# Small products of the attention weights moved to quarters of the array, regrouped through memory

## Chip, cores, metric

One core of a Trainium2 chip. The metric is the device time of one execution in microseconds (us). Every number below is from a run or a profile; a number worked out from others says how. Engines in the profile: PE (matmul), PEld (its weight loads), DVE (vector), ACT (scalar), POOL, and SP, whose queue (SPq) issues nearly all transfers. PSUM is the memory that the matmuls of this kernel write to; it is handed out in banks, here often in pairs. A transfer has landed when the semaphore that reports its end is complete.

## The reference

Two linear-attention blocks A and B read the same input `x` (2048 x 640), each with 32 heads of 20 columns; a sigmoid gate mixes them.

```python
qkv = (x @ wqkv) ...                      # per block: q, k, v
pq, pk = phi(q), phi(k)                   # phi(t) = where(t > 0, t + 1, exp(t)) + 1e-6
kv  = einsum("bhsd,bhse->bhde", pk, v)    # 20 x 20 per head
num = einsum("bhqd,bhde->bhqe", pq, kv);  den = einsum("bhqd,bhd->bhq", pq, z)[..., None] + 1e-6
a   = (num / den) ... @ wo
return g * a + (1 - g) * b
```

## The kernel before

Since `num @ wo` is `pq @ (kv @ wo)`, the kernel makes W' = blockdiag(kv) @ wo (640 x 640) once per block. The output is then pq, scaled by gate over denominator, times W', summed over both blocks. PE runs, in this order: K of both blocks; the Gram products G of A, with Q products as filler; G of B, with Q products, **kv and W' of A** as filler; partial sums of A (one per 128 rows of output, "o_part"), with **kv and W' of B** among them; then the products with W' of B ("o_rest") and the last rows.

The parts that matter (cuts marked `# ...`):

```python
GR = 120; NU = 6                       # six heads = 120 rows; six units per block
def kv_unit(X):                        # kv of six heads in one 120x120 block, then masked to the block diagonal
    for us in ((0, 1, 2, 3), (4, 5)):
        # PE: 5 matmuls per unit, moving 120 columns each
        # DVE: KVL[:, us, (m g)] = PS[:, (u g m)] * mask        (one copy for 4 units, one for 2)
def wp_unit(X, u):                     # one unit of W': 120 rows x 640 columns
    ps = Buf("wp", "ps", 2)            # one pair of PSUM banks
    e.matmul(a[0:GR, 0:512], KVL[X][:, u, :], WO[X][:, u, 0:512], start=True, stop=True)
    e.matmul(a[0:GR, 512:D], KVL[X][:, u, :], WO[X][:, u, 512:D], start=True, stop=True)
    # ins=[bkvl[X][u // 4], ...]: waits for its own masked copy only
    # ACT copies the 120 x 640 result to WST, then one transfer spreads it over WP:
    dma("SP", ..., WP[X][lo // 5 : hi // 5, :, :], WST[X][r:GR, u, :], ...)
# ...
o_part(0); o_part(1); o_part(2); den("B"); o_part(3); kv_unit("B"); o_part(4)
for u in range(NU):
    wp_unit("B", u)
    if u % 2 == 0: o_part(5 + u // 2)
for t in range(8, NOA): o_part(t)      # NOA = 13
for t in range(NOA): o_rest(t)         # first use of W' of B
```

All engines are driven by a small scheduler in the kernel: PE keeps the order of the program, and the order on DVE, ACT and the queue comes from a simulation with modelled costs. Each engine then runs its list strictly in order. `den` makes the denominators: per 512 rows a transfer with transpose, three DVE steps (reduce, reciprocal, factor) and a transpose back.

Of the kernel before, what the change touches and what calls it, by code (L numbers as in the profile page):

```python
# [11 lines left out]
D = 640  # L12
# [7 lines left out]
NU = 6  # L20

# [7 lines left out]
def _consts():  # L29
    p = np.arange(128)[:, None]  # L30
    bd = (p // 20 == np.arange(24)[None, :] // 4).astype(np.float32)
    return _bf16_bits(bd)


CW = 24
# [4 lines left out]
class Buf:  # L40


    def __init__(self, name, pool=None, n=1):
        self.name, self.pool, self.n = name, pool, n
        self.writers, self.readers = [], []
        self.slot = None
        self.war = []
# [25 lines left out]
class Sched:  # L73
# [14 lines left out]
    def run(self):  # L88
# [10 lines left out]
        def can(o, t):  # L99

            w = t
            if o.behind is not None and o.behind.start is None:
                return None
            for d in o.deps:
                if d.end is None:
                    return None
                w = max(w, d.end + (HOP if d.eng != o.eng or d.dma else 0.0))
            for b in o.outs:
                if b.pool and b.slot is None:
                    got = self.pick(b, w)  # L110
                    if got is None:
                        return None
                    w = max(w, got[0])
            return w

        n = len(self.ops)
        while len(self.order) < n:
# [25 lines left out]
            if o.dma:  # L143
                at[e] = w + o.dma[0]
                o.end = max(w + o.dma[0] + 1500.0, bus[0]) + o.dma[1] / o.dma[2]
                bus[0] = o.end
            else:
                o.end = at[e] = w + o.cost
                if e == "PE":
                    o.end += 160.0  # L150
# [14 lines left out]
    def pick(self, b, t):  # L165
# [3 lines left out]
        for x in pool:  # L169
            have[x[1]] = x[0]  # L170
        if b.n == 1:
            if not pool:
                return None
# [3 lines left out]
        c = [(max(have[s], have[s + 1]), s) for s in have if s % 2 == 0 and s + 1 in have]  # L177
# [80 lines left out]
def body(nc, A_x, A_wqkv, A_wo, B_x, B_wqkv, B_wo, gate_w, out, log=None):  # L258
# [17 lines left out]
    WV = {X: sb("WV" + X, [128, NC, D], bf) for X in XS}  # L276
    WO = {X: sb("WO" + X, [GR, NU, D], bf) for X in XS}
# [19 lines left out]
    KVL = {X: sb("KVL" + X, [GR, NU, GR], bf) for X in XS}  # L297
    WST = {X: WKW[0:GR, i * NU * D : (i + 1) * NU * D].rearrange("p (u f) -> p u f", u=NU) for i, X in enumerate(XS)}
# [5 lines left out]
    NOA = 13  # L304
    OA = [XNf[:, 2048 + 1280 * i : 3328 + 1280 * i].bitcast(f32) for i in range(6)]
    OA += [PK["B"][:, 1280 * i : 1280 * i + 1280].bitcast(f32) for i in range(7)]
# [22 lines left out]
    BDM = CST[0:GR, 0:24]  # L329
# [9 lines left out]
    def dma(q, name, dst, src, nbytes, ins=(), outs=(), after=(), issue=450.0, transpose=False, prio=None):  # L339
        def fn(e):  # L340
# [4 lines left out]
        o = op(q, fn, 0.0, ins, outs, after, prio=prio, name=name, dma=(issue, nbytes, 95.0 if transpose else 330.0))  # L345
# [24 lines left out]
    bwo = {X: Buf("wo" + X) for X in XS}  # L370
# [15 lines left out]
    zgw = op("POOL", lambda e: e.memset(GWZ[:, :], 0.0), 200.0, name="zgw")  # L386
    bxo = Buf("xo")
# [8 lines left out]
    def xt_dma(t0, t1):  # L396
# [7 lines left out]
            issue=(t1 - t0) * 850.0,  # L404
# [22 lines left out]
    for X in XS:  # L427
        dma("SP", "wv" + X, WV[X][:, :, :], w3(X, 2), 819200, outs=[bwv[X]])
    for X in XS:
        bo5 = Buf("wo5" + X)  # L430
        dma("SP", "wo" + X, WO[X][:, 0:5, :], wo[X][0:600, :].rearrange("(u p) n -> p u n", p=GR), 768000, outs=[bwo[X]])
        dma("SP", "wo5" + X, WO[X][:, 5, :], wo[X][520:640, :], 153600, outs=[bo5])
        bwo[X, 5] = bo5
# [176 lines left out]
    def g_unit(X, g, fill):  # L610
        ps = Buf("g", "ps", 2)
        i = XS.index(X)
        for t in range(NT):
# [30 lines left out]
            issue=850.0,  # L644
# [6 lines left out]
    def kv_unit(X):  # L651
        gv = GS[X][:, :, :].rearrange("p c (g m) -> p c g m", g=NC)
        for us in ((0, 1, 2, 3), (4, 5)):
            ps = Buf("kv", "ps")

            def fn(e, us=us, ps=ps):
                for i, u in enumerate(us):
                    lo = GR * u if u < 5 else D - GR
                    for c in range(NC):
                        r = e.matmul(  # L660
                            PS[0:GR, ps.slot, GR * i : GR * i + GR],
                            WV[X][:, c, lo : lo + GR],
                            gv[:, c, :, lo // 5 : lo // 5 + 24],
                            start=(c == 0),
                            stop=(c == NC - 1),
                        )
                return r

            o = op("PE", fn, 5 * len(us) * mm_cost(GR), ins=[bwv[X]] + [bgs[X, g] for g in range(NC)], outs=[ps], name="kv" + X)
            if X == "A":  # L670
                kv_op[X].append(o)
            b = Buf("kvl")
            bkvl[X].append(b)
            n = len(us)
            op(
                "DVE",
                lambda e, us=us, ps=ps, n=n: e.tensor_tensor(
                    out=KVL[X][:, us[0] : us[0] + n, :].rearrange("p u (m g) -> p u g m", g=NC),
                    in0=PS[0:GR, ps.slot, 0 : GR * n].rearrange("p (u g m) -> p u g m", u=n, g=NC),
                    in1=BDM.unsqueeze(1).unsqueeze(1).to_broadcast([GR, n, NC, 24]),  # L680
                    op=ALU.mult,
                ),
                dve1(GR * n),
# [6 lines left out]
    bwp = {}  # L690
    bwpm = {X: [] for X in XS}

    def wp_unit(X, u):
        ps = Buf("wp", "ps", 2)

        def fn(e):
            a = psw(ps, D)
            e.matmul(a[0:GR, 0:512], KVL[X][:, u, :], WO[X][:, u, 0:512], start=True, stop=True)  # L698
            return e.matmul(a[0:GR, 512:D], KVL[X][:, u, :], WO[X][:, u, 512:D], start=True, stop=True)  # L699

        op(
            "PE",
            fn,
            mm_cost(512) + mm_cost(128),
            ins=[bkvl[X][u // 4], bwo[X] if u < 5 else bwo[X, 5]],
            outs=[ps],
            name="wp%s%d" % (X, u),
        )
        b = Buf("wst")
        op(  # L710
            "ACT",
            lambda e: e.activation(WST[X][:, u, :], psw(ps, D)[0:GR, :], ACT.Copy),
            act_cost(D),
            ins=[ps],
            outs=[b],
            prio=-1,
            name="wpc",
        )
        bwp[X, u] = b
        d = Buf("wpm")  # L720
        bwpm[X].append(d)
        r = 80 if u == 5 else 0
        lo, hi = GR * u, min(D, GR * u + GR)
        dma(
            "SP",
            "wpm%s%d" % (X, u),
            WP[X][lo // 5 : hi // 5, :, :],
            WST[X][r:GR, u, :],
            1280 * (hi - lo),
            ins=[b],  # L730
            outs=[d],
            issue=850.0,
            prio=-1,
        )
# [85 lines left out]
    def den(X):  # L820

        i = XS.index(X)
        for b in range(NB):
# [10 lines left out]
                issue=900.0,  # L834
# [40 lines left out]
                issue=900.0,  # L875
# [112 lines left out]
    def fill_b(g):  # L988
        def f(k):
# [14 lines left out]
            elif g == 2:  # L1004
                q_next(1)
                wp_unit("A", 2 * k)
                wp_unit("A", 2 * k + 1)
            elif g == 3:
                q_next(2)
# [12 lines left out]
    den("B")  # L1022
    o_part(3)
    kv_unit("B")
    o_part(4)
    for u in range(NU):
        wp_unit("B", u)
        if u % 2 == 0:
            o_part(5 + u // 2)
# [52 lines left out]
```

## Time and profile before

| | before |
|---|---|
| median time, first three runs | 188.76 us |
| PE busy | 98% of the span |
| PE waits in all | 0.7 us |
| W' on PE, both blocks | 12 units of 0.27 us = 3.3 us |
| kv on PE | 30 matmuls, 1.65 us per block |

First the page: span, busy time by engine, then the busy tenths and the granted PE clock in 40 equal slices, then the chain that ended last.

```profile
span 187.6 us, 3202 instructions
PE 184.6 (98%) x1261; PEld 107.9 (58%) x1261; DVE 135.4 (72%) x260; ACT 95.6 (51%) x171; POOL 0.8 (0%) x8
...
PE   8999999999999999999999999999999999999995
...
PEclk9999999999999999999999999999999999999999
...
PE 96%; DMA 2%; SPq 0%; DVE 0%; issue 0%; DVEq 0%
```

PE is the limit from end to end, at full clock (9 means 90% or more; the mean of this profile is 1.000). A gain must take time out of PE's stream, and any new wait of PE is a loss. The view of waits for PE confirms it: columns are who waited, for whom, total us, times, longest.

```profile
PE ps L444 <- DVE ONE L372: 0.4, 1, 0.4
PE ps L513 <- DMA WKW<-in_A_wqkv_dram: 0.3, 1, 0.3
```

The timeline of PE around the first W' unit of B (start us, duration us, engine, line, operation):

```profile
147.00 0.38 PE L698 MATMUL ps<-WOB,KVLB 120*120 120x512 bf16 x1
147.22 0.22 PE L699 MATMUL ps<-WOB,KVLB 120*120 120x128 bf16 x1
147.27 0.65 PE L904 MATMUL ps<-WPA,EX 128*128 128x512 bf16 x3
```

Durations overlap in the pipeline, so the cost of a unit is read from starts: 147.27 - 147.00 = 0.27 us.

The masked copies of kv of B on DVE, and the issue times of the six transfers that spread W' of B (minimum, median, maximum ns; first and last start):

```profile
L677 DVE TENSOR_TENSOR KVLB<-ps,CST x2: 908/1204/1499, 145.3 to 146.5; 120x480 bf16<-120x480 f32 x1, 120x240 bf16<-120x240 f32 x1
...
L343 SPq DMA_DIRECT2D WPB<-WKW x6: 689/772/792, 150.1 to 155.5; - x6
```

### The profile page before, as it was taken

Reading aid. Unit: us, or ns where it says so; the run is one execution under the profiler, and the core shown is the slowest. Engines: PE = TensorE matmul, PEld = TensorE weight load, DVE = VectorE, ACT = ScalarE, POOL = GpSimd, SP = SyncE. Lnnn points to the kernel's source line nnn. Section 1 sums busy time; section 2 is a strip of 40 time slices with the busy share of each in tenths; the row PEclk is TensorE's granted clock in tenths of the full one; section 3 lists DMA queues with packets and bytes.
Section 4 is the critical chain, followed back from the end, with each engine's and each line's share of the span. In section 5 each row is a group of like instructions: output and inputs, shape, how many; then the busy total and the mean of one; then the engine's idle time right before and its main releaser. Section 6 shows DMA issues by size and latency. Waiting matters only on the chain.

```text
span 187.6 us, 3202 instructions
## 1 busy us (share of the span) xinstructions
PE 184.6 (98%) x1261; PEld 107.9 (58%) x1261; DVE 135.4 (72%) x260; ACT 95.6 (51%) x171; POOL 0.8 (0%) x8
## 2 busy tenths in 40 slices
PE   8999999999999999999999999999999999999995
PEld 4555555555555656665557556655556655555552
DVE  2388888888833555487798999879996999965600
ACT  5365655556554546544675667877524594100012
POOL 1000000000000000000000000000000000000000
PEclk9999999999999999999999999999999999999999
DMA  7999999996001011011701222540015165132322
GB/s 185 293 163 158 252 392 364 344 214 136 4 0 35 0 38 35 0 35 24 92 10 31 56 49 48 124 116 3 0 35 118 32 153 134 39 140 105 136 79 70
DMA packets 36301, 19.89 MB, mean 106 GB/s; under 512 B 25630, under 2 KB 36286, under 8 KB 36286
## 3 DMA queue, kind: packets, MB, share of 16 engines
q1 hardware_dynamic: 35844, 19.48, 41.6%
q8 instruction: 10, 0.16, 0.4%
q10 hardware_dynamic: 442, 0.20, 0.4%
q14 instruction: 5, 0.04, 0.1%
HBM read 9.39 MB, written 2.62 MB: 64 GB/s over the span
## 4 chain that ended last, share of the span: by engine, by line
PE 96%; DMA 2%; SPq 0%; DVE 0%; issue 0%; DVEq 0%
PE ps L904 23%; PE ps L744 23%; PE ps L513 18%; PE ps L618 18%; PE ps L619 5%; PE ps L514 5%; DMA WKW<-in_A_wqkv_dram 2%; PE ps L660 2%; PE ps L698 1%; SPq L343 0%; PE ps L699 0%; DVE TSB L948 0%; DVEq L230 0%; PE ps L494 0%
## 5 line engine op out<-in xcount | busy, mean ns | idle before, releaser
L513 PE MATMUL ps<-WKW,XT 128*128 128x512 bf16 x160 | 44.4, 381 | 0.3 <-DMA WKW<-in_A_wqkv_dram 0.3
L761 ACT ACTIVATE EK<-ps 128x512 bf16<-128x512 f32 x40 | 23.9, 598 | 31.5 <-PE ps L744 29.4
L514 PE MATMUL ps<-WKW,XT 128*128 128x128 bf16 (+1 forms) x160 | 35.2, 220 | 0.0
L546 ACT ACTIVATE EK<-ps 128x640 bf16<-128x640 f32 x32 | 22.4, 704 | 10.8 <-DVE EK L549 5.9
L513 PEld LDWEIGHTS ps<-WKW,XT 128*128 128x128 bf16 x160 | 15.7, 98 | 19.8 <-DMA WKW<-in_A_wqkv_dram 0.6
L744 PE MATMUL ps<-XT,WQA 128*128 128x512 bf16 x100 | 24.5, 379 | 0.0
L744 PE MATMUL ps<-XT,WQB 128*128 128x512 bf16 x100 | 23.7, 379 | 0.0
L618 PE MATMUL ps<-XN,PKB 128*128 128x512 bf16 x80 | 23.5, 379 | 0.0
L618 PE MATMUL ps<-XN,PKA 128*128 128x512 bf16 x80 | 23.5, 379 | 0.0
L771 DVE TENSOR_SCALAR EK<-EK 128x512 bf16<-128x512 bf16 x40 | 11.6, 291 | 14.9 <-ACT EK L761 14.8
L619 PE MATMUL ps<-XN,PKA 128*128 128x129 bf16 x80 | 17.6, 220 | 0.0
L619 PE MATMUL ps<-XN,PKB 128*128 128x129 bf16 x80 | 17.6, 220 | 0.0
L904 PE MATMUL ps<-WPA,EX 128*128 128x512 bf16 x120 | 17.3, 299 | 0.0
L904 PE MATMUL ps<-WPB,PKA 128*128 128x512 bf16 x120 | 16.5, 299 | 0.0
L744 PEld LDWEIGHTS ps<-XT,WQB 128*128 128x128 bf16 x100 | 10.9, 117 | 8.5
L514 PEld LDWEIGHTS ps<-WKW,XT 128*128 128x128 bf16 x160 | 15.8, 98 | 0.0
L549 DVE TENSOR_SCALAR EK<-EK 128x640 bf16<-128x640 bf16 x32 | 10.4, 326 | 7.1 <-ACT EK L546 7.1
L744 PEld LDWEIGHTS ps<-XT,WQA 128*128 128x128 bf16 x100 | 10.6, 117 | 8.1
L618 PEld LDWEIGHTS ps<-XN,PKA 128*128 128x128 bf16 x80 | 9.4, 118 | 7.9
L618 PEld LDWEIGHTS ps<-XN,PKB 128*128 128x128 bf16 x80 | 9.4, 117 | 7.8
L950 ACT ACTIVATE TSB<-ps 128x640 bf16<-128x640 f32 (+1 forms) x3 | 2.0, 668 | 23.2 <-PE ps L904 23.2
L557 DVE SCALAR_TENSOR_TENSOR PKA<-ps,EK 128x640 bf16<-128x640 f32 x16 | 13.2, 825 | 0.6
(77 smaller groups left out, 239.9 us busy)
## 6 DMA issues: line engine op xcount, KB each, us to landing
out_dram<-TSB SPq DMA_DIRECT2D x15, 160.0 KB, 1.8
XN<-in_A_x_dram SPq DMA_DIRECT2D x1, 2240.0 KB, 9.0
WKW<-in_A_wqkv_dram SPq DMA_DIRECT2D x5, 160.0 KB, 4.2
WKW<-in_B_wqkv_dram SPq DMA_DIRECT2D x5, 160.0 KB, 4.0
WQA<-in_A_wqkv_dram SPq DMA_DIRECT2D x1, 800.0 KB, 10.7
WQB<-in_B_wqkv_dram SPq DMA_DIRECT2D x1, 800.0 KB, 11.9
WVA<-in_A_wqkv_dram SPq DMA_DIRECT2D x1, 800.0 KB, 12.7
WVB<-in_B_wqkv_dram SPq DMA_DIRECT2D x1, 800.0 KB, 14.3
```

Source lines behind the costliest of these rows:

```text
L513: e.matmul(a[:, 0:512], l, WK[X][:, c, 0:512], start=(c == 0), stop=(c == NC - 1))
L514: return e.matmul(a[:, 512:w], l, WK[X][:, c, 512:w], start=(c == 0), stop=(c == NC - 1))
L546: op("ACT", lambda e: e.activation(EK[:, ek.slot, :], psw(ps, D), ACT.Exp), act_cost(D), ins=[ps] + first, outs=[ek], name="ke")
L549: lambda e: e.tensor_scalar(EK[:, ek.slot, :], EK[:, ek.slot, :], 1.0, EPS, op0=ALU.min, op1=ALU.add),
L557: lambda e: e.scalar_tensor_tensor(PKt[X][:, t, :], psw(ps, D), 0.0, EK[:, ek.slot, :], op0=ALU.max, op1=ALU.add),
L618: e.matmul(a[:, 0:512], l, XN[:, t, 0:512], start=(t == 0), stop=(t == NT - 1))
L619: return e.matmul(a[:, 512 : D + 1], l, XN[:, t, 512 : D + 1], start=(t == 0), stop=(t == NT - 1))
L660: r = e.matmul(PS[0:GR, ps.slot, GR * i : GR * i + GR], WV[X][:, c, lo : lo + GR], gv[:, c, :, lo // 5 : lo // 5 + 24], start=(c == 0), st ...
L744: r = e.matmul(PS[:, ps.slot, :], WQ[X][:, c, g::5], XT[:, c, 512 * b : 512 * b + 512], start=(c == 0), stop=(c == NC - 1),)
L761: lambda e: e.activation(EQ[:, eq.slot, :], PS[:, ps.slot, :], ACT.Exp),
L771: lambda e: e.tensor_scalar(EQ[:, eq.slot, :], EQ[:, eq.slot, :], 1.0, EPS, op0=ALU.min, op1=ALU.add),
L904: r = e.matmul(a[:, l0 - lo : h0 - lo], PQ[X, b][:, g, 128 * (t % 4) : 128 * (t % 4) + 128], WP[X][:, g, l0:h0], start=(X == first and g = ...
```

## The change

Three heads at a time need only a 60 x 60 block of kv, so four such products fit on the four 64 x 64 quarters of the array at once. W' is made in two bursts per block, each with half the columns of all eleven products (ten of 60 rows, one of 40). `wo` is loaded at offsets 4 and 64 to fit the quarters, with zero padding. Since a quarter holds 60 rows, the eleven pieces are no longer spread one by one: five stores write W' to memory, and one load brings it back in the layout of WP. Fourteen partial sums of A are kept instead of 13, to give PE more to do while W' of B travels. The scheduling model gets other numbers for transposes.

```diff
+HR = 60; HALF = 320
-        o = op(..., dma=(issue, nbytes, 95.0 if transpose else 330.0))          # and issue=850.0 or 900.0 for transposes
+        timing = (330.0, 1500.0) if not transpose else (140.0, 1500.0) if loading else (1000.0, 1150.0)   # and issue=1250.0
-    NOA = 13
+    NOA = 14
 # kv: WV padded to 128 columns per unit; the sixth unit moves 40 columns instead of 120; three masked copies (480, 120, 40 columns)
+    def wp_burst(X, half):
+        ps = [Buf("wp", "ps", 2) for _ in range(2)]          # two pairs of banks at once
+        for k in range(3):
+            for a, b in ((0, 192), (192, HALF)) if k == 1 else ((0, HALF),):
+                for t in range(4 * k, min(4 * k + 4, 11)):
+                    c, r, u = t // 2 % 2, t % 2 if t < 10 else 1, t // 2
+                    # matmul on quarter (row half r, column half c)
+        op("PE", fn, 640.0, ins=bkvl[X] + ..., outs=ps)      # waits for all three masked copies
+        # two ACT copies of 124 x 960; after the second burst 2 + 3 stores (st), then:
+            dma("SP", "wpl" + X, WP[X][:, :, :], WPD[X].rearrange("(p g) n -> p g n", g=NC), 819200, ins=bwps[X], ...)
-    o_part(3); kv_unit("B"); o_part(4); six wp_units among o_part(5) to o_part(7)
+    kv_unit("B"); o_part(3); wp_burst("B", 0); o_part(4); o_part(5); wp_burst("B", 1); o_part(6); o_part(7)
 # ... (padding, memsets on POOL, split loads of wo, PSUM picking for two pairs)
```

More of the change, by code (lines that the diff above doesn't have):

```diff
@@ L20 @@
 NU = 6
+HR = 60
+HALF = 320
 def _bf16_bits(a):
@@ L30, in _consts @@
     p = np.arange(128)[:, None]
-    bd = (p // 20 == np.arange(24)[None, :] // 4).astype(np.float32)
-    return _bf16_bits(bd)
-CW = 24
+    q, m = p % 64, np.arange(24)[None, :]
+    bd = np.where(p < 64, (q >= 4) & ((q - 4) // 20 == m // 4), (q < 60) & (3 + q // 20 == m // 4))
+    be = q // 20 == m[:, 0:8] // 4
+    return _bf16_bits(np.concatenate([bd, be], axis=1).astype(np.float32))
+CW = 32
 XS_W = 672
@@ L40, with __init__ @@
 class Buf:
-    def __init__(self, name, pool=None, n=1):
-        self.name, self.pool, self.n = name, pool, n
+    def __init__(self, name, pool=None, n=1, at=(0, 2, 4, 6)):
+        self.name, self.pool, self.n, self.at = name, pool, n, at
         self.writers, self.readers = [], []
@@ L107, in can @@
                 w = max(w, d.end + (HOP if d.eng != o.eng or d.dma else 0.0))
+            skip = set()
             for b in o.outs:
                 if b.pool and b.slot is None:
-                    got = self.pick(b, w)
+                    got = self.pick(b, w, skip)
                     if got is None:
@@ L113, in can @@
                     w = max(w, got[0])
+                    skip |= set(range(got[1], got[1] + b.n))
             return w
@@ L144, in run @@
                 at[e] = w + o.dma[0]
-                o.end = max(w + o.dma[0] + 1500.0, bus[0]) + o.dma[1] / o.dma[2]
+                o.end = max(w + o.dma[0] + o.dma[3], bus[0]) + o.dma[1] / o.dma[2]
                 bus[0] = o.end
@@ L163, in run, with pick @@
         return max(o.end for o in self.ops)
-    def pick(self, b, t):
+    def pick(self, b, t, skip=()):
         pool = self.free[b.pool]
@@ L169, in pick @@
         for x in pool:
-            have[x[1]] = x[0]
+            if x[1] not in skip:
+                have[x[1]] = x[0]
         if b.n == 1:
-            if not pool:
+            if not have:
                 return None
@@ L176, in pick @@
             return best[0], best[3]
-        c = [(max(have[s], have[s + 1]), s) for s in have if s % 2 == 0 and s + 1 in have]
+        c = [(max(have[i] for i in range(s, s + b.n)), s) for s in b.at if all(i in have for i in range(s, s + b.n))]
         return min(c) if c else None
@@ L275, in body @@
     WQ = {X: sb("WQ" + X, [128, NC, D], bf) for X in XS}
-    WV = {X: sb("WV" + X, [128, NC, D], bf) for X in XS}
-    WO = {X: sb("WO" + X, [GR, NU, D], bf) for X in XS}
+    WV = {X: sb("WV" + X, [128, NC, D + 8], bf) for X in XS}
+    WO = {X: sb("WO" + X, [128, NU, D], bf) for X in XS}
     PK = {X: sb("PK" + X, [128, NT * D], bf) for X in XS}
@@ L296, in body @@
     GS = {X: sb("GS" + X, [128, NC, D], bf) for X in XS}
-    KVL = {X: sb("KVL" + X, [GR, NU, GR], bf) for X in XS}
-    WST = {X: WKW[0:GR, i * NU * D : (i + 1) * NU * D].rearrange("p (u f) -> p u f", u=NU) for i, X in enumerate(XS)}
+    KVL = {X: sb("KVL" + X, [128, NU, GR], bf) for X in XS}
+    WST = {X: WKW[:, i * NU * D : (i + 1) * NU * D].rearrange("p (u f) -> p u f", u=NU) for i, X in enumerate(XS)}
     WP = {X: sb("WP" + X, [128, NC, D], bf) for X in XS}
@@ L303, in body @@
     FXT = {"A": WV["A"][:, :, :].rearrange("p c f -> p (c f)")[:, 0:2048].rearrange("p (b s) -> p b s", b=NB), "B": XNf[:, 0:2048].rearrange("p (b s) -> p b s", b=NB)}
-    NOA = 13
+    NOA = 14
     OA = [XNf[:, 2048 + 1280 * i : 3328 + 1280 * i].bitcast(f32) for i in range(6)]
-    OA += [PK["B"][:, 1280 * i : 1280 * i + 1280].bitcast(f32) for i in range(7)]
+    OA += [PK["B"][:, 1280 * i : 1280 * i + 1280].bitcast(f32) for i in range(8)]
     NEK, NEQ, NOS = 4, 4, 4
@@ L328, in body @@
     IDN = sb("IDN", [128, 128], bf)
-    BDM = CST[0:GR, 0:24]
+    BDM = CST[:, 0:24]
+    BDE = CST[64:104, 24:32]
     sch = Sched({"ps": 8, "ek": NEK, "eq": NEQ, "os": NOS})
@@ L343, in fn @@
                 return e.dma_start(d, src() if callable(src) else src, transpose=transpose)
-        o = op(q, fn, 0.0, ins, outs, after, prio=prio, name=name, dma=(issue, nbytes, 95.0 if transpose else 330.0))
+        o = op(q, fn, 0.0, ins, outs, after, prio=prio, name=name, dma=(issue, nbytes) + timing)
         if loading:
@@ L369, in body @@
     bwv = {X: Buf("wv" + X) for X in XS}
-    bwo = {X: Buf("wo" + X) for X in XS}
+    bwo = {}
     op("DVE", lambda e: e.memset(ONE[:, :], 1.0), 120.0, outs=[bone], name="one")
@@ L386, in body @@
     zgw = op("POOL", lambda e: e.memset(GWZ[:, :], 0.0), 200.0, name="zgw")
+    bpad = {X: Buf("pad") for X in XS}
+    for X in XS:
+        op("POOL", lambda e, X=X: e.memset(WV[X][:, :, 0:4], 0.0), 100.0, outs=[bpad[X]], prio=10**6, name="wvpad")
+        op("POOL", lambda e, X=X: e.memset(WO[X][0:4, 0:5, :], 0.0), 1500.0, outs=[bpad[X]], prio=10**6, name="wopad")
     bxo = Buf("xo")
@@ L403, in xt_dma @@
             outs=bxt[t0:t1],
-            issue=(t1 - t0) * 850.0,
+            issue=(t1 - t0) * 1250.0,
             transpose=True,
@@ L427, in body @@
     for X in XS:
-        dma("SP", "wv" + X, WV[X][:, :, :], w3(X, 2), 819200, outs=[bwv[X]])
+        dma("SP", "wv" + X, WV[X][:, :, 4 : D + 4], w3(X, 2), 819200, outs=[bwv[X]])
     for X in XS:
-        bo5 = Buf("wo5" + X)
-        dma("SP", "wo" + X, WO[X][:, 0:5, :], wo[X][0:600, :].rearrange("(u p) n -> p u n", p=GR), 768000, outs=[bwo[X]])
-        dma("SP", "wo5" + X, WO[X][:, 5, :], wo[X][520:640, :], 153600, outs=[bo5])
-        bwo[X, 5] = bo5
+        for r in range(2):
+            bwo[X, r] = Buf("wo")
+            dma(
+                "SP",
+                "wo%s%d" % (X, r),
+                WO[X][4 + HR * r : 64 + HR * r, 0:5, :],
+                wo[X][0:600, :].rearrange("(u r p) n -> r p u n", r=2, p=HR)[r],
+                384000,
+                outs=[bwo[X, r]],
+            )
+        bwo[X, 2] = Buf("wo")
+        dma("SP", "wo2" + X, WO[X][64:104, 5, :], wo[X][600:640, :], 51200, outs=[bwo[X, 2]])
     loading.clear()
@@ L643, in g_unit @@
             outs=[bgs[X, g]],
-            issue=850.0,
+            issue=1250.0,
             transpose=True,
@@ L652, in kv_unit, with out @@
         gv = GS[X][:, :, :].rearrange("p c (g m) -> p c g m", g=NC)
-        for us in ((0, 1, 2, 3), (4, 5)):
-            ps = Buf("kv", "ps")
-            def fn(e, us=us, ps=ps):
-                for i, u in enumerate(us):
-                    lo = GR * u if u < 5 else D - GR
-                    for c in range(NC):
-                        r = e.matmul(
-                            PS[0:GR, ps.slot, GR * i : GR * i + GR],
-                            WV[X][:, c, lo : lo + GR],
-                            gv[:, c, :, lo // 5 : lo // 5 + 24],
-                            start=(c == 0),
-                            stop=(c == NC - 1),
-                        )
-                return r
-            o = op("PE", fn, 5 * len(us) * mm_cost(GR), ins=[bwv[X]] + [bgs[X, g] for g in range(NC)], outs=[ps], name="kv" + X)
-            if X == "A":
-                kv_op[X].append(o)
+        def out(src, u0, n, w, mask, r0, r1):
             b = Buf("kvl")
             bkvl[X].append(b)
-            n = len(us)
             op(
                 "DVE",
-                lambda e, us=us, ps=ps, n=n: e.tensor_tensor(
-                    out=KVL[X][:, us[0] : us[0] + n, :].rearrange("p u (m g) -> p u g m", g=NC),
-                    in0=PS[0:GR, ps.slot, 0 : GR * n].rearrange("p (u g m) -> p u g m", u=n, g=NC),
-                    in1=BDM.unsqueeze(1).unsqueeze(1).to_broadcast([GR, n, NC, 24]),
+                lambda e: e.tensor_tensor(
+                    out=KVL[X][r0:r1, u0 : u0 + n, 0 : w * NC].rearrange("p u (m g) -> p u g m", g=NC),
+                    in0=src().rearrange("p (u g m) -> p u g m", u=n, g=NC),
+                    in1=mask.unsqueeze(1).unsqueeze(1).to_broadcast([r1 - r0, n, NC, w]),
                     op=ALU.mult,
                 ),
-                dve1(GR * n),
+                dve1(w * NC * n),
                 ins=[ps, bcst],
@@ L688, in kv_unit, with fn @@
             )
-    bwp = {}
-    bwpm = {X: [] for X in XS}
-    def wp_unit(X, u):
-        ps = Buf("wp", "ps", 2)
-        def fn(e):
-            a = psw(ps, D)
-            e.matmul(a[0:GR, 0:512], KVL[X][:, u, :], WO[X][:, u, 0:512], start=True, stop=True)
-            return e.matmul(a[0:GR, 512:D], KVL[X][:, u, :], WO[X][:, u, 512:D], start=True, stop=True)
-        op(
-            "PE",
-            fn,
-            mm_cost(512) + mm_cost(128),
-            ins=[bkvl[X][u // 4], bwo[X] if u < 5 else bwo[X, 5]],
-            outs=[ps],
-            name="wp%s%d" % (X, u),
-        )
-        b = Buf("wst")
-        op(
-            "ACT",
-            lambda e: e.activation(WST[X][:, u, :], psw(ps, D)[0:GR, :], ACT.Copy),
-            act_cost(D),
-            ins=[ps],
-            outs=[b],
-            prio=-1,
-            name="wpc",
-        )
-        bwp[X, u] = b
-        d = Buf("wpm")
-        bwpm[X].append(d)
-        r = 80 if u == 5 else 0
-        lo, hi = GR * u, min(D, GR * u + GR)
+        for us in ((0, 1, 2, 3), (4, 5)):
+            ps = Buf("kv", "ps")
+            def fn(e, us=us, ps=ps):
+                for i, u in enumerate(us):
+                    for c in range(NC):
+                        lo, n, w = (GR * u, 128, 24) if u < 5 else (540, 104, 8)
+                        r = e.matmul(
+                            PS[0:n, ps.slot, GR * i : GR * i + NC * w],
+                            WV[X][:, c, lo : lo + n],
+                            gv[:, c, :, 24 * u : 24 * u + w],
+                            start=(c == 0),
+                            stop=(c == NC - 1),
+                        )
+                return r
+            o = op("PE", fn, 5 * len(us) * 55.0, ins=[bwv[X], bpad[X]] + [bgs[X, g] for g in range(NC)], outs=[ps], name="kv" + X)
+            if X == "A":
+                kv_op[X].append(o)
+            n = min(us[-1], 4) - us[0] + 1
+            out(lambda ps=ps, n=n: PS[:, ps.slot, 0 : GR * n], us[0], n, 24, BDM, 0, 128)
+            if 5 in us:
+                out(lambda ps=ps: PS[64:104, ps.slot, GR : GR + 40], 5, 1, 8, BDE, 64, 104)
@@ new lines, in body @@
+    bwst = {(X, r): Buf("wst") for X in XS for r in range(2)}
+    bwps = {X: [] for X in XS}
+    WPD = {X: nc.dram_tensor("wps" + X, [D, D], bf, kind="Internal").ap() for X in XS}
+    bwpm = {X: [Buf("wpm")] for X in XS}
+    def wp_burst(X, half):
+        ps = [Buf("wp", "ps", 2) for _ in range(2)]
+        lo = HALF * half
+        def fn(e):
+            for k in range(3):
+                for a, b in ((0, 192), (192, HALF)) if k == 1 else ((0, HALF),):
+                    for t in range(4 * k, min(4 * k + 4, 11)):
+                        c, r, u = t // 2 % 2, t % 2 if t < 10 else 1, t // 2
+                        w, p = (64 - 4 * r, HR) if t < 10 else (40, 40)
+                        d = HR * r if t < 10 else 0
+                        o = PS[64 * c : 64 * c + p, ps[r].slot : ps[r].slot + 2, :].rearrange("p a b -> p (a b)")
+                        x = e.matmul(
+                            o[:, HALF * k + a : HALF * k + b],
+                            KVL[X][64 * r : 64 * r + w, u, d : d + p],
+                            WO[X][64 * r : 64 * r + w, u, lo + a : lo + b],
+                            start=True,
+                            stop=True,
+                        )
+            return x
+        op("PE", fn, 640.0, ins=bkvl[X] + [bwo[X, i] for i in range(3)] + [bpad[X]], outs=ps, name="wp%s%d" % (X, half))
+        for r in range(2):
+            op(
+                "ACT",
+                lambda e, r=r: e.activation(
+                    WST[X][0:124, 3 * r : 3 * r + 3, lo : lo + HALF],
+                    psw(ps[r], 3 * HALF)[0:124, :].rearrange("p (k n) -> p k n", k=3),
+                    ACT.Copy,
+                ),
+                act_cost(3 * HALF),
+                ins=[ps[r]],
+                outs=[bwst[X, r]],
+                prio=-1 if X == "A" else None,
+                name="wpc",
+            )
+            if half == 0:
+                continue
+            for c in range(2):
+                st(X, r, c, 3 * r, 2 if c else 3, HR, 120 * c + HR * r)
+            if r:
+                st(X, r, 2, 5, 1, 40, 600)
+        if half == 1:
+            dma("SP", "wpl" + X, WP[X][:, :, :], WPD[X].rearrange("(p g) n -> p g n", g=NC), 819200, ins=bwps[X], outs=bwpm[X], prio=-1)
@@ L724, in wp_unit, with st @@
+    def st(X, r, c, slot, n, rows, row):
+        h = 64 * min(c, 1)
+        b = Buf("wps")
+        bwps[X].append(b)
         dma(
             "SP",
-            "wpm%s%d" % (X, u),
-            WP[X][lo // 5 : hi // 5, :, :],
-            WST[X][r:GR, u, :],
-            1280 * (hi - lo),
-            ins=[b],
-            outs=[d],
-            issue=850.0,
+            "wps%s%d%d" % (X, r, c),
+            bass.AP(tensor=WPD[X].tensor, offset=WPD[X].offset + D * row, ap=[[D, rows], [240 * D, n], [1, D]]),
+            WST[X][h : h + rows, slot : slot + n, :],
+            1280 * rows * n,
+            ins=[bwst[X, r]],
+            outs=[b],
+            issue=450.0,
@@ L833, in den @@
                 after=[red_op[b]] if b in red_op else (),
-                issue=900.0,
+                issue=1250.0,
                 transpose=True,
@@ L874, in den @@
                 after=kv_op[X],
-                issue=900.0,
+                issue=1250.0,
                 transpose=True,
@@ L1004, in f @@
             elif g == 2:
+                if k == 2:
+                    wp_burst("A", 1)
                 q_next(1)
-                wp_unit("A", 2 * k)
-                wp_unit("A", 2 * k + 1)
+                if k == 0:
+                    wp_burst("A", 0)
             elif g == 3:
@@ L1022, in body @@
     den("B")
+    kv_unit("B")
     o_part(3)
-    kv_unit("B")
+    wp_burst("B", 0)
     o_part(4)
-    for u in range(NU):
-        wp_unit("B", u)
-        if u % 2 == 0:
-            o_part(5 + u // 2)
+    o_part(5)
+    wp_burst("B", 1)
+    o_part(6)
+    o_part(7)
     for t in range(8, NOA):
```

## The prediction

> **What bounds the kernel now.** The page gives a span of 187.6 us with PE (matmul) busy 98%, granted clock full in all 40 slices. The chain that ended last is 96% PE; in the view of waits PE waits 0.7 us in all. So two things count: PE time, and new waits of PE. DVE, 72% overall, is over 80% busy from 138 to 159.5 us (table of stretches).
>
> **Removed.** W' is 6 units per branch, a 512- and a 128-column matmul each; in the timeline a unit moves the stream on by 0.27 us (147.00 to 147.27). 12 units are 3.3 us, all on the critical path. kv takes 30 matmuls at 55 ns, 1.65 us per branch.
>
> **Added on PE.** Per branch two bursts of 15 matmuls on quarters. The Trainium skill ("TensorEngine Tiling (Array Packing)", Key Properties) says that tiles run in parallel and that a change of tiling mode drains the array. No run here shows quarters yet. Perfectly parallel, a burst streams 960 columns: 0.40 us at this trace's rate (512 columns in 0.216). At the 55 ns per load-and-matmul pair of kv, 15 pairs are 0.83 us. I take 0.7 with drains, an estimate: four bursts 2.8 us, gain 0.45. The sixth kv unit shrinks from 120 to 40 columns: gain about 0.15.
>
> **New wait 1: masking kv, branch B.** The first W' unit needs only the first masked copy today; a burst needs all three. Today's two last 1.50 us (480 columns) and 0.91 us (240); a line through these gives about 0.6 for 120 and 0.4 for 40 (estimate). kv would start near 142.6; the first copy starts 1.3 us after it, as today; the three end near 146.5. PE has one partial product (1.36 us) to fill with, done at 145.5. Expected stall 1.0 us. In A the burst comes over 10 us after kv: no stall.
>
> **New wait 2: W' of B through memory.** After the second burst PE has 8 partial products, 10.9 us. In them: two ACT copies of 960 columns (about 1.0 us each, from 0.60 for 512 and 0.70 for 640), perhaps one partial-sum copy before (0.7); the last three stores' issues (0.33 to 0.77 us each, as output stores and today's regrouping); landing of a store 1.8 us (median of outputs); an 800 KB load, about 4 us (1.8 plus 819 KB at the page's peak slice, 392 GB/s: an estimate); perhaps a transpose issue (1.2 us) between. Sum 9 to 12 us: mostly slack, perhaps a stall of up to 1 us; I take 0.1. In A there is over 10 us of slack.
>
> **Neutral.** 14 instead of 13 kept sums: equal PE work, one more DVE add where DVE is 30% free. Padding memsets lie on idle POOL.
>
> **Predicted time.** 188.76 - 0.45 - 0.15 + 1.0 + 0.1 = 189.3; as the other engines' order changes in ways I haven't traced and the author may have filled the first stall, I say 188.9 us, 187.3 to 190.6.
>
> **What would show each step.** A burst on PE 0.6 to 0.9 us; near 0.4 quarters overlap fully, near 1.5 they don't. Wait view: B's first burst waits about 1 us for DVE's masked copies; the first B product waits 0 to 1 us for the W' load. kv near 1.55 us. No PE wait in A. The load lands about 4 us after issue.
>
> **What would make it wrong.** Quarters run one after another (+2.6 us), or far cheaper (-1.2); masked copies ordered behind reciprocals (0.95 us each more); transposes issued ahead of stores (1.2 each); no free PSUM pairs for a burst's four banks; or masked copies much shorter or filled: then 188.

## The result, and the profile after

| | before | after |
|---|---|---|
| median of six runs, same rounds | 188.81 us (188.38 to 189.23) | 189.64 us (189.33 to 190.13) |
| ratio, 95% interval | | 1.0046 (1.0025 to 1.0068) |

All runs were fast. Ratios here are the mean time of one kernel's fast runs over that of the other's of the same rounds, so not quite the ratio of the medians quoted. The time is 0.8 us longer.

The page of after, the same lines:

```profile
span 188.4 us, 3250 instructions
PE 182.7 (97%) x1273; PEld 106.8 (57%) x1297; DVE 136.5 (72%) x263; ACT 95.4 (51%) x167; POOL 6.2 (3%) x12
...
PE 76%; DVE 15%; DMA 5%; issue 2%; ACT 1%; SPq 0%; DVEq 0%; ACTq 0%
```

PE has less work, but the chain now leaves PE for 24% of the span. (PE's busy sum is also short of 24 matmul records, 1273 for 1297 weight loads; they show as gaps of one matmul and cost no time.) The view of waits for PE names three new waits:

```profile
PE ps L736 <- DVE ZC L652: 0.8, 1, 0.8
PE ps L736 <- DVE KVLB L681: 0.5, 1, 0.5
PE ps L953 <- DMA WPB<-wpsB: 0.5, 1, 0.5
PE ps L466 <- DVE ONE L382: 0.4, 1, 0.4
```

L736 is a burst, L953 an output product. The first wait is in A, the other two in B. The timeline of PE around the first burst of B, and its masked copies on DVE:

```profile
144.48 1.30 PE L953 MATMUL ps<-WPA,EX 128*128 128x128 bf16 x9
146.26 0.60 PE L736 MATMUL ps<-WOB,KVLB 64*60 64x320 bf16 x15 [0.47 <-DVE KVLB L681]
146.80 0.66 PE L953 MATMUL ps<-WPA,EX 128*128 128x512 bf16 x3
```

```profile
L681 DVE TENSOR_TENSOR KVLB<-ps,CST x3: 273/574/1487, 144.0 to 145.8; 128x480 bf16<-128x480 f32 x1, 128x120 bf16<-128x120 f32 x1, 40x40 bf16<-40x40 f32 x1
```

The quarters overlap nearly fully: the first four matmuls of this burst start at 146.260, 146.264, 146.267 and 146.270 us, and PE goes on 0.54 us after the burst's start. Where nothing else holds a burst, it starts 0.09 us later than the matmul before it allows. So a burst costs 0.63 us, against three units at 0.27.

The same two facts for the queue: issue times of the stores (wpsB) and the load (WPB), and from issue to landing (minimum, median, maximum us; the maximum is the load).

```profile
L353 SPq DMA_DIRECT2D wpsB<-WKW x5: 423/592/728, 151.4 to 153.7; - x5
L353 SPq DMA_DIRECT2D WPB<-wpsB x1: 462/462/462, 157.2 to 157.2; - x1
...
DMA to landing us min/median/max: 2.8/3.0/4.4
```

The stores had all landed at 156.50 us. The load was issued at 157.17, behind two transposes (issued from 154.49 and 155.74), and landed at 161.53; PE went on at 161.67.

To compare runs I took PE's starts from each trace: for the first burst of A (in kernels with units: the first unit), the first burst of B and the first product with W' of B, the gap beyond what the matmul before it needs. A burst's gap includes the 0.09 us of entering quarters. "Stream" is from the first Gram matmul to the last matmul of the kernel; it leaves out the load phase, whose end lay between 48.02 and 48.69 us in the profiles of all kernels, in no relation to the edits.

| profiled run | gap A | gap B | gap load | stream us | median us |
|---|---|---|---|---|---|
| before | 0.00 | 0.00 | 0.00 | 136.75 | 188.81 |
| after | 0.93 | 0.64 | 0.64 | 137.86 | 189.64 |

The accounts: waits of 0.84 + 0.55 + 0.64 = 2.03 us (0.09 taken off the first two) against a stream longer by 1.11. So PE's own work fell by about 0.9 us; from the starts it is 12 x 0.272 - 4 x 0.66 = 0.62 for W' (0.63 and 0.03 of a slower first matmul behind it) and 0.24 for kv (1.65 to 1.53 us per block; about half of it from the 25 matmuls of 120 columns, which follow each other after 52.5 ns instead of 55). The profiled run of after had a load phase 0.3 us shorter, hence the span's 0.8.

### The profile page after: what moved, and what is told of

The parts are those of the page before. It is cut to its first block, busy times and chain, and to the rows that moved or that the text cites. A ratio compares the mean times of both kernels' runs of the same rounds, so it can differ in the third digit from the quotient of the medians.

```text
span 188.4 us, 3250 instructions
## 1 busy us (share of the span) xinstructions
PE 182.7 (97%) x1273; PEld 106.8 (57%) x1297; DVE 136.5 (72%) x263; ACT 95.4 (51%) x167; POOL 6.2 (3%) x12
## 4 chain that ended last, share of the span: by engine, by line
PE 76%; DVE 15%; DMA 5%; issue 2%; ACT 1%; SPq 0%; DVEq 0%; ACTq 0%
PE ps L535 18%; PE ps L793 18%; PE ps L640 14%; PE ps L953 13%; PE ps L536 5%; PE ps L641 4%; DVE TSB L854 3%; DMA TTR<-TSH 3%; DVE DNT L900 3%; DMA WPB<-wpsB 2%; DVE FF L903 2%; DVE DNT L888 2%; PE ps L466 1%; DVE KVLB L681 1%; DVE EK L820 1%
## 5 line engine op out<-in xcount | busy, mean ns | idle before, releaser
L535 PE MATMUL ps<-WKW,XT 128*128 128x512 bf16 x154 | 43.7, 385 | 0.0
L793 PE MATMUL ps<-XT,WQA 128*128 128x512 bf16 x96 | 24.0, 379 | 0.1
L953 PE MATMUL ps<-WPB,PKA 128*128 128x512 bf16 (+1 forms) x118 | 16.4, 298 | 0.6 <-DMA WPB<-wpsB 0.5
L953 PE MATMUL ps<-WPA,EX 128*128 128x512 bf16 (+1 forms) x117 | 16.5, 297 | 0.3 <-issue 0.2
L579 DVE SCALAR_TENSOR_TENSOR PKB<-ps,EK 128x640 bf16<-128x640 f32 x16 | 13.2, 825 | 0.6
```

The costliest lines, as they stand in the source:

```text
L535: e.matmul(a[:, 0:512], l, WK[X][:, c, 0:512], start=(c == 0), stop=(c == NC - 1))
L579: lambda e: e.scalar_tensor_tensor(PKt[X][:, t, :], psw(ps, D), 0.0, EK[:, ek.slot, :], op0=ALU.max, op1=ALU.add),
L793: r = e.matmul(PS[:, ps.slot, :], WQ[X][:, c, g::5], XT[:, c, 512 * b : 512 * b + 512], start=(c == 0), stop=(c == NC - 1),)
L953: r = e.matmul(a[:, l0 - lo : h0 - lo], PQ[X, b][:, g, 128 * (t % 4) : 128 * (t % 4) + 128], WP[X][:, g, l0:h0], start=(X == first and g = ...
```

## The experiments

**My theory:** PE's work did fall, and three separate waits took back more than that. **Rivals:** DVE is the real limit from 100 to 160 us, and PE's waits only show it; the new order of the other engines, from the new model numbers, made the loss by itself; the trip through memory is too long whatever is done around it. Twelve kernels ran.

### Take each wait away, then all three

**e1_zc_first.** A burst needs two PSUM pairs at once. In after, one of them was still held by the Gram accumulator of B until DVE's last small read of it (L652), and DVE did three denominator steps first:

```profile
112.99 0.69 DVE L888 TENSOR_REDUCE DNT<-TTR 128x128 f32<-128x512 bf16 x1 [0.28 <-DMA TTR<-TSH]
113.71 0.95 DVE L900 RECIPROCAL DNT<-DNT 128x128 f32<-128x128 f32 x1
114.70 0.69 DVE L903 TENSOR_TENSOR FF<-DNT,GG 128x512 bf16<-128x512 f32 x1
115.42 0.16 DVE L652 COPY ZC<-ps 128x1 f32<-128x1 f32 x1
```

```diff
             outs=[z],
+            prio=-1,
             name="zc",
```

> The copy of the denominator column that frees the accumulator's PSUM pair goes first on DVE. Theory (the first burst of A waits 0.84 us for a PSUM pair which that copy holds): the wait before the first burst of A falls below 0.1 us and the first partial product starts about 0.8 us earlier than in the changed kernel (138.66 us there); time about 188.8, the changed kernel's 189.64 less 0.8, unless the later waits in B grow. Rival (DVE is the real limit between 100 and 160 us, PE waits only show it): the wait moves on to B's mask or to another DVE result, and under 0.3 us is gained.

**e2_split_deps.** The first two thirds of a burst use only the first masked copy.

```diff
-        op("PE", fn, 640.0, ins=bkvl[X] + ..., outs=ps, ...)
+        for ks, kb in (((0, 1), bkvl[X][0:1]), ((2,), bkvl[X])):
+            op("PE", lambda e, ks=ks: fn(e, ks), 640.0 * len(ks) / 3, ins=kb + ..., outs=ps, ...)
```

> Each burst is two PE steps; the first two thirds wait only for the first masked copy, the last third for all three. Theory (the first burst of B waits 0.55 us because it needs all three copies): the wait before it falls to about 0.1 us, plus up to 0.2 us inside the burst; but the later wait for the W' load (0.62 us) ends later than PE by less, since the load follows the second burst, so the whole gains about 0.3 to 0.5 us: 189.2. Rival (DVE-bound): no gain in all.

**e3_load_first.**

```diff
+            if X == "B":
+                for b in (2, 3):
+                    ft_op[b].deps.append(o)        # the last two transposes of factors after the load o
```

> The last two transposes of B's factors are issued after the W' load instead of before it. Theory (the load was held on the queue by them for about 0.6 us after the last store had landed, and landed later): the load is issued within 0.2 us of the last store's landing, the first product with W' of B waits under 0.1 us instead of 0.62; time about 189.0. Rival (the trip through memory itself is too long): the wait stays above 0.4 us.

**e4_all_three.** The three edits together.

> The three edits together. Theory (three separate waits of 0.84, 0.55 and 0.62 us hide a saving of 1.0 us of PE time): time about 187.7 to 188.0, that is 0.8 to 1.0 us below the kernel before, PE waits under 0.4 us after 100 us. Rival (DVE-bound between 100 and 160 us): within 0.3 us of the kernel before or slower.

| profiled run | gap A | gap B | gap load | stream us | median us | ratio (95%) |
|---|---|---|---|---|---|---|
| e1 | 0.09 | 0.63 | 1.20 | 137.57 | 190.74 | 1.0074 (1.0040 to 1.0108) |
| e2 | 0.77 | 0.09 | 2.54 | 139.22 | 190.86 | 1.0081 (1.0047 to 1.0116) |
| e3 | 0.54 | 0.63 | 0.95 | 137.77 | 189.77 | 1.0048 (1.0031 to 1.0065) |
| e4 | 0.09 | 0.09 | 0.34 | 136.36 | 188.39 | 0.9978 (0.9959 to 0.9997) |

(The before of these rounds: 188.86 us.) Each of e1 and e2 removed the wait it aimed at, and neither gained time in the runs: the wait for the load grew, by 0.56 of the 0.84 us in e1, which left its stream 0.29 shorter, and by 1.90 against 0.55 in e2. My expectation of separate gains failed. In e1 all of B came about 0.6 us earlier (the first store at 150.76 against 151.40), but the scheduler had now put a third transpose between the stores; it took the queue from 151.86 to 153.27, so the load was issued at 157.12, as in after (157.17). In e2 PE came 0.5 us earlier to its second burst of B, but the last transpose before the stores only 0.1; the load was issued at 157.03, the issue itself took 1.63 us against 0.46 in after, and it landed 5.9 us after its start:

```profile
L353 SPq DMA_DIRECT2D WPB<-wpsB x1: 1633/1633/1633, 157.0 to 157.0; - x1
...
DMA to landing us min/median/max: 5.9/5.9/5.9
```

Two of e1's six runs and one of e2's were slow, at a mean granted clock of 0.991; these count in the medians, not in the ratios.

e3 did issue the load 0.07 us after the last store had landed (156.33 after 156.26). But that load took 5.6 us to land:

```profile
L353 SPq DMA_DIRECT2D WPB<-wpsB x1: 353/353/353, 156.3 to 156.3; - x1
...
DMA to landing us min/median/max: 2.8/3.0/5.6
```

So the queue's order was a part of this wait, and the load's own time another. In these four runs it landed 4.3 (e1) to 5.9 us (e2) after its issue.

Only all three together gave a gain over before, of 0.2% with an interval that ends just below 1, and a smaller one than expected (187.7 to 188.0). The rival "DVE is the limit" also fails as I stated it: the wait went on to the load and not to a DVE result. But it holds in one respect: the transposes that share the queue are released by DVE's denominator steps, and in e2 they hardly moved with PE (0.1 us against 0.5). e6 below shows the same from the other side.

### Which part of the change makes which wait?

**e5_before_model.** The kernel before with only the new model numbers (diff: the `timing` and `issue` lines above).

> The kernel before with only the changed numbers of the scheduling model (how long transposes take), so only the order on DVE, ACT and the queue can differ. Theory (bursts and the trip through memory make the loss): within 0.3 us of the kernel before and no PE wait over 0.2 us. Rival (the new order alone made waits): 0.5 us or more slower, with a wait in A near 114 us or in B near 145 us.

Gaps: 0.00 at the first unit of A, 0.00 in B, 0.00 at the load; stream 137.42; 189.56 us against 188.62, ratio 1.0044 (1.0024 to 1.0064). The rival was right here: PE waited 0.6 us beyond the matmul's own time at the *second* unit of A, for the same small read of the accumulator. In the view of waits, which counts only from the modelled end of the matmul before:

```profile
PE ps L700 <- DVE ZC L632: 0.4, 1, 0.4
```

**e11_old_model.** The changed kernel with the old model numbers.

> The changed kernel with the old numbers of the scheduling model, so the other engines' order is built as in the kernel before. Theory A (the new order made the wait of A, as in the run of the order alone, where 0.61 us stood at the same place): the first burst of A waits under 0.2 us, the first partial product starts 0.6 to 0.8 us earlier than the changed kernel's; the mask and load waits stay within 0.4 us of 0.55 and 0.62; time about 189.0. Theory B (the burst's need of two PSUM pairs at once made it): the wait stays at 0.5 us or more.

Gap A 0.09: theory A holds, the wait of A comes from the order and not from the burst's two pairs. But gap B stays 0.65 and the load's grows to 1.85; stream 138.24, 190.53 us against 188.85, ratio 1.0103 (1.0072 to 1.0134); one of its six runs, of 192.19 us, had a clock of 0.991 and still counts as fast. My 189.0 was wrong because the time gained in A was waited away again, as in e1. The second burst of B was 0.8 us earlier than in after (148.83 against 149.62 us), the first store only 0.07 (151.33 against 151.40): it stood behind a transpose issued from 150.09 to 151.28. The load then stood behind two more, took 0.99 us to issue and landed at 161.96.

### Is the trip through memory the trouble, and is there another way?

**e9_before_memory.** The kernel before with its six units; only the six spreading transfers replaced by three stores and one load.

```diff
-        dma("SP", "wpm%s%d" % (X, u), WP[X][lo // 5 : hi // 5, :, :], WST[X][r:GR, u, :], ...)
+        if u in (2, 5): ...      # stores of units 0 to 2, 3 to 4 and 5 to memory
+        if u == NU - 1:
+            dma("SP", "wpl" + X, WP[X][:, :, :], WPD[X].rearrange("(p g) n -> p g n", g=NC), 819200, ins=bwps[X], ...)
```

> The kernel before, its six units kept, with W' regrouped through memory by three stores and one load. Theory (the trip costs two landings in series, about 3 and 4.4 us and issue time): W' of B lands near 162 us where PE needs it at 159.5: one new wait of 2 to 3.5 us, time 191 to 192.5. Rival (fewer transfers on the queue make up for it): under 1 us slower.

Gap of the load 3.19 us (one lost record, 0.22, taken off), stream 141.62, 192.81 us against 188.62, ratio 1.0211 (1.0166 to 1.0257), which by the 2% rule is unclear. The load landed at 162.19, as I said. This is the trip in its queue's order and not alone: the third store stood behind a transpose (153.18 to 155.89) and landed at 157.82, 0.8 us after the second, so up to 0.8 of the 3.19 us may be the transpose's. The time rose by more than the gap, and above the 192.5 I allowed. The table of stretches shows why (stretch, its length, busy us of each engine, then PEclk, DMA share, GB/s):

```profile
159.00:162.50 3.50, 0.29 (x3) 0.13 (x2) 2.28 (x4) 0.70 (x1) 0.00 (x0) 1.00 0.60 223
162.50:164.00 1.50, 1.46 (x10) 0.81 (x10) 0.09 (x1) 0.00 (x0) 0.00 (x0) 0.89 0.00 0
164.00:167.00 3.00, 3.00 (x13) 1.50 (x12) 1.16 (x2) 0.00 (x0) 0.00 (x0) 0.50 0.18 60
167.00:170.00 3.00, 3.00 (x24) 1.64 (x23) 1.60 (x3) 0.00 (x0) 0.00 (x0) 0.99 0.16 58
```

After PE's long wait the granted clock fell to 0.50, for 3.4 us in all with the parts in the stretches before and after (0.89 of 1.50 us and 0.99 of 3.00), which is 1.7 us more; with the gap of 3.19 that is about the 4.87 us by which the stream grew. The Trainium skill ("TensorE: Matmul & The Clock Gate", What's actually happening) says that an idle window of about 3.4 us on a free-running grid halves the clock. This trace shows the halving, but after a wait of 3.2 us, shorter than that window; and the clock fell about 1.1 us after PE had gone on. e2's profile, with a wait of 2.5 us, kept 1.00. Of e9's four runs, the two at clock 0.991 took 193.45 and 194.12 us, the two at 1.0 took 192.16 and 191.93. The slow runs of e1 and e2 have the same 0.991; whether they too waited that long is not known, since they have no trace.

**e7_direct.** The bursts kept, each piece spread directly, so 11 transfers instead of five stores and a load.

```diff
+        for i in range(n):
+            dma("SP", ..., WP[X][p0 : p0 + rows // 5, :, :], WST[X][h : h + rows, slot + i, :], 1280 * rows, ...)
```

> The changed kernel with its bursts, but W' regrouped by 11 direct transfers (60 or 40 rows each) instead of five stores and one load through memory. Theory (the trip through memory, two landings in series, ends after PE needs W' of B): the last piece lands by about 159.5 us, the first B product waits under 0.1 us instead of 0.62, time about 189.0; the waits of A (0.84) and of the mask (0.55) stay. Rival (11 issues on one queue cost more than they save): the last piece lands after 161 us and the wait stays or grows.

**e8_direct_best.** The same with the edits of e1 and e2.

> The same with the PSUM copy first and the split dependencies of the bursts. Theory: no PE wait over 0.15 us after 100 us; PE work saved (1.0 us) shows in full: about 187.7 us, 1.0 to 1.2 below the kernel before. Rival (DVE-bound): above 188.4.

| profiled run | gap A | gap B | gap load | stream us | median us | ratio (95%) |
|---|---|---|---|---|---|---|
| e7 | 0.56 | 0.64 | 1.64 | 138.49 | 190.44 | 1.0097 (1.0076 to 1.0118) |
| e8 | 0.09 | 0.09 | 1.99 | 138.00 | 189.99 | 1.0066 (1.0049 to 1.0084) |

(The before of these rounds: 188.62 us.) My theory fell and the rival was right: the last piece landed at 161.93 (e7) and 161.53 us (e8). A transfer of 60 rows costs the queue as much as one of 120 did:

```profile
L353 SPq DMA_DIRECT2D WPB<-WKW x11: 682/765/785, 150.8 to 159.0; - x11
```

I had taken half of that for half the bytes. Eleven issues are 8.8 us of queue. This is what the quarters bring with them: pieces half as tall, so twice as many. Through memory the five stores took 3.1 us of queue, but two landings in series. Neither way fits into the time that PE leaves, as the queue is ordered here. Issuing a part of these transfers from another engine's queue was not tried.

### More for PE to do, and the mask

**e10_noa15.** One more partial sum of A before W' of B is needed.

```diff
-    NOA = 14
+    NOA = 15
+    OA += [XT[:, :, :].rearrange("p c s -> p (c s)")[:, 0:1280].bitcast(f32)]
```

> The changed kernel with 15 instead of 14 partial sums of A (the fifteenth kept in the space of the transposed input), so PE has one more product of 1.36 us to do before it needs W' of B. Nothing on the queue is touched. Theory (PE reaches the first B product before the load lands): the wait of 0.62 us falls below 0.1; time about 189.0. Rival (DVE or the queue is the limit and moves the load by as much): the wait stays.

Gaps 0.66, 0.63, 0.78; stream 137.72; 189.77 us against 188.85, ratio 1.0046 (1.0031 to 1.0062). It missed: the load of this run was issued at 156.86 and took 5.9 us, to 162.78, so the wait came back. With after's 4.4 us there would have been none (estimate: 156.86 + 4.36 = 161.22, while PE was ready at about 162.1).

**e6_mask_contig.** Wrong result (relative error 0.38): the masked copies write contiguously.

```diff
-out=KVL[X][r0:r1, u0 : u0 + n, 0 : w * NC].rearrange("p u (m g) -> p u g m", g=NC),
+out=KVL[X][r0:r1, u0 : u0 + n, 0 : w * NC].rearrange("p u (g m) -> p u g m", g=NC),
```

> Wrong result on purpose: the masked copies write their columns contiguously instead of in steps of five elements. If the step of ten bytes is what makes the 480-column copy take 1.49 us, it takes 0.6 to 0.8 us here and the first burst of B waits under 0.1 us instead of 0.55. If it is the broadcast mask or the short runs of 24, it stays above 1.3 us.

```profile
L681 DVE TENSOR_TENSOR KVLB<-ps,CST x3: 203/272/657, 143.5 to 144.4; 128x480 bf16<-128x480 f32 x1, 128x120 bf16<-128x120 f32 x1, 40x40 bf16<-40x40 f32 x1
```

The 480-column copy falls from 1.49 to 0.66 us; the step of five elements in the output was the cost. The gap of B falls to 0.09. One run of 188.99 us, with a load gap of 0.83. More than the mask's wait changed: the three copies together took 1.2 us less of DVE per block, the gap of A fell to 0.16, the load was issued at 155.78 (157.17 in after) and landed at 160.71, and the stream was 136.73, as long as before's. So less work on DVE alone made the stream 1.13 us shorter than after's, where removing one of PE's waits (e1, e2) did not: a sign for the rival, but from one run.

**e12_all_noa15.** The edits of e4 and e10 together.

> PSUM copy first, split dependencies, load ahead of the transposes, and 15 partial sums. Theory: no PE wait over 0.15 us after 100 us, span 0.3 us shorter than with 14 partial sums in the same version (186.93), about 188.1 us, 0.6 to 0.9 below the kernel before, and runs within 0.6 us of each other. Rival: DVE's added sum or the tail costs what the wait did, 188.4 or more.

Gaps 0.09, 0.09, 0.00; stream 136.00; 188.20 us (187.76 to 188.61) against 188.85, ratio 0.9967 (0.9951 to 0.9983). All that is left in the view of waits for PE:

```profile
PE ps L467 <- DVE ONE L383: 0.4, 1, 0.4
```

The load landed at 160.90 us, 5.0 us after its issue, and the first product with W' of B started at 161.66, so there is some slack even for a slow landing. The stream is 0.75 us shorter than before's and 0.36 shorter than e4's; the span, 187.0, did not show the latter, as this profile had the longest load phase (48.69 us against e4's 48.26). This version is 0.3% faster than the kernel before, and about 0.8% faster than the changed kernel (from the two ratios, 1.0046 and 0.9967; other rounds). That it is faster than e4 is seen in the stream only; their ratios overlap. The range of its runs, 0.85 us, was wider than the 0.6 I expected.

## Why the prediction was right

The time (188.9 said, 189.64 measured) held, and its two opposed parts are real. Term by term:

- **Bursts: said 0.7 us each, gain 0.45; measured 0.63 to 0.66, gain 0.62.** The quarters do overlap. The Trainium skill ("TensorEngine Tiling (Array Packing)", Key Properties) says that tiles run in parallel and that changing the mode drains the array: this trace shows the first four starts 3 to 4 ns apart, and 0.09 us on entering. After a burst PE goes on 0.09 us later than the last matmul's 320 columns need.
- **kv: said 0.15, measured 0.24.** The five matmuls of 40 columns per block, which I had counted on, give 0.05 us per block; the other 25, on weights padded from 120 to 128 columns, give 0.06, which I had not seen.
- **Mask wait: said 1.0, measured 0.55.** The mechanism was right. The term was mis-sized: the three copies took 2.10 us together where I had about 2.5 (the small ones 0.57 and 0.27 instead of 0.6 and 0.4, and the second began 0.25 us before the first had ended), and PE left its last partial product 0.1 us later than I put it. e2 and e6 each remove this wait.
- **Load wait: said 0 to 1, taken as 0.1; measured 0.64.** The landing of a store took about 3 us where I had 1.8 (the outputs' median), and the transposes stood before the load. That the load itself varies from 4.3 to 5.9 us, I had not foreseen.
- **"In A the burst comes over 10 us after kv: no stall" failed: 0.84 us.** I looked only at kv, and listed PSUM pairs as a bare risk. The cause was an accumulator released late by DVE's new order, which e5 shows without any burst, e11 by taking the new order away, and e1 by moving one 0.16 us copy.
- I reduced the sum of +0.5 to +0.1 because the author "may have filled the first stall". He had not; the undiscounted 189.3 was nearer.
- **Luck.** Two errors in the kernel's favour (PE's work 0.26 us better than said, the mask wait 0.45 shorter) made up for about half of the two against it (0.84 in A, not in the sum at all, and 0.54 more at the load). The time lay in the range partly for that reason.

My reading of the slack was wrong in kind. I treated the waits as separate. In e1, e2 and e11 PE came 0.5 to 0.8 us earlier to its second burst of B, and W' of B, whose stores share a queue with transposes released by DVE, still landed at 161.5 to 162.9 us. Most or all of the time saved ahead of that point was then waited away. It landed sooner where that path itself was eased: at 160.09 in e4, with the load ahead of the transposes, and at 160.71 in e6, with less work on DVE. What stays open is why the load took 4.3 us in one run and 5.9 in another: it ranged from 4.3 to 5.9 with transposes in flight (e1, e2) and from 4.6 to 5.6 without (e4, e3). The traces narrow it. A load's semaphore counts 16 steps. In e3, e10 and e12 fifteen of them had come within 4.5 us of the issue and the last one only at 5.6, 5.9 and 5.0; in e2 the issue itself took 1.63 us. So in these runs it is one late share, or a long issue, and not a slower transfer as a whole; what holds the late share is not shown.

## What to carry to other kernels

A product that is made four times as dense saves its own time only if everything that must be ready at once (all masked copies, two PSUM pairs) and everything that must follow (half-sized pieces to be spread) still fits; cost these first. Where PE is never idle, look for the last point at which a result comes back from a slower path: here saving PE time ahead of that point was worth little or nothing (e1, e2) until that path got shorter as well (e4) and more filler was put before it (e12). When a scheduler's model is changed along with an idea, run the model change alone: here it made a loss of the size of the whole change on the kernel before (e5), although taking it out of the changed kernel made that one no faster (e11), so its effect does not simply add.

## What the Trainium skill lacked or had wrong

- "TensorEngine Tiling (Array Packing)", Key Properties, gives no size for the drain on a mode change: 0.09 us on entering a burst and 0.09 on leaving it here.
- "SBUF — State Buffer", Door 1, says that lines of 16 bytes let one stride over up to 8 bf16 elements for free, and also that full bandwidth needs two hits per line, which steps of 5 elements (10 bytes) miss; it gives no size of the penalty. Here a DVE copy that writes bf16 in steps of 5 elements took 1.49 us for 480 columns, and 0.66 us with step 1 (one run), so a step below 8 was not free for this copy.
- "DMA: Bandwidth & Descriptors", Where the ~2 µs actually goes, calls descriptor generation a small cost, for transfers issued from GpSimd. No page was found that gives, by shape, how long an issue from SP holds its queue. Here a spreading transfer held it for 0.77 us, with 120 rows as with 60.
- No page was found that gives the spread of one and the same load: 800 KB from memory landed 4.3 to 5.9 us after issue over ten profiled runs.
